# Sparse attention into a mixture of experts: loads in order of use, slots in two steps, a check moved, banks rotated

## The chip, the cores and the metric

The kernel runs on one core of one Trainium2 chip. The metric is the device time of one execution in microseconds (us): the median over several runs. The profile comes from one more execution, and its span is counted from the first to the last instruction of the program. TensorE (PE) multiplies matrices, VectorE (DVE) and ScalarE (ACT) work elementwise, GpSimd (POOL) issues gathers and scatters by index, and SyncE (SP) issues the plain transfers (DMA). PSUM, where TensorE writes, has 8 banks of 512 fp32 per partition.

## The reference

Attention of 8 batches, 8 heads, 576 positions and 64 values a head. Half of the heads look at the last 32 positions, the other half at earlier positions of the same remainder modulo 32. Its output is the input of a mixture of 8 experts, of which each token takes one:

```
scores = scale * q @ k.T;  scores = where(mask_local or mask_strided, scores, -1e9)
attn   = exp(scores - max);  attn /= sum(attn) + 1e-9;  x = attn @ v     # (8, 576, 512)
logits = x @ w_gate;  local_gate = sigmoid(x @ w_local)
for b in range(8):
    prev_e = -1
    for s in range(576):
        fresh_e = argmax(logits[b, s])
        e = fresh_e if s == 0 or local_gate[b, s] < 0.5 else prev_e
        prev_e = e
        p = softmax(logits[b, s])
        out[b, s] = p[e] * (relu(x[b, s] @ w1[e]) @ w2[e])     # w1[e]: 512 x 1024, w2[e]: 1024 x 512
```

The choice of an expert can depend on the token before it, so it is made by a scan along the tokens.

## The kernel before

The kernel has three stages. Attention works through 32 pairs of heads (8 batches of 4 pairs): scores, exponential, mask, values, then transposes for the gate. The tokens of the first three batches are routed while attention goes on ("route" with nb = 3), and six tiles of 128 tokens of them can start early as soon as attention ends. During those tiles ("early") all eight batches are routed (nb = 8); the rest follows in pairs of tiles. TensorE, VectorE, ScalarE, GpSimd and SyncE each work through their own list in order; a scheduler fixes these orders when the program is built, and `issue_after` keeps an instruction behind another one.

Queries, keys and values of a batch come in two groups of two pairs each. The queries and keys of the very first pair come in pieces; everything else of a group comes whole:

```python
    def load(b, grp):
        hs = slice(2 * grp, 2 * grp + 2)
        qt = inp.tile([P, 2, S], F32, name="qt")
        kt = inp.tile([P, 2, KW], F32, name="kt")
        if b == grp == 0:

            hq, hk = LT // 2 * LQ, LT // 2 * LQ + STRIDE
            for c, d in ((slice(0, hq), slice(0, hk)), (slice(hq, S), slice(hk, KW))):
                nc.sync.dma_start(out=qt[:, 0, c], in_=q[b][:, hs][:, 0, c])
                nc.scalar.dma_start(out=kt[:, 0, d], in_=k[b][:, hs][:, 0, d])
        a = slice(int(b == grp == 0), 2)
        nc.sync.dma_start(out=qt[:, a], in_=q[b][:, hs][:, a])
        nc.sync.dma_start(out=kt[:, a], in_=k[b][:, hs][:, a])
        st["q", b, grp], st["k", b, grp] = qt, kt
        if grp == 0:
            t = inp.tile([LK, 2, LT, VW], F32, name="vlt", bufs=2)
            nc.sync.dma_start(out=t, in_=vl[b])
        else:
            t = inp.tile([P, 2, len(SBLK), VW], F32, name="vst", bufs=2)
            nc.sync.dma_start(out=t, in_=vs[b])
        st["v", b, grp] = t

    def blocks(ap, m):
        return ap.rearrange("p h (i x) -> p h i x", i=m)
# ... cut: scores, values, transposes, gates ...
    pairs = [[Unit(b, pair, g) for g in range(2)] for b in range(B) for pair in range(PAIRS)]
    load(0, 0)
    load(0, 1)
    nc.sync.dma_start(out=wgs, in_=wg.rearrange("(k p) e -> p k e", p=P))
```

In each step n of the attention the scores of pair n are made, then route may take a step, and then come the values of pair n - 1 and the transposes of pair n - 2. Route is a generator; each `yield` gives way to the attention or the experts. Its part from the slots on (a slot is a token's place in the experts' tiles; `slot` has a row for each batch and expert, 24 or 64 of them, and a column for each position):

```python
    nc.vector.tensor_scalar(slot, cum, thr, float(SKIP), Alu.is_le if final else Alu.is_gt, Alu.mult)
    nc.vector.scalar_tensor_tensor(slot, cum, base, slot, Alu.add, Alu.add)
# ... cut ...
    nc.vector.tensor_tensor(slot, slot, hot, op=Alu.mult)
    yield


    ps = bank()
    ones = PAIR_MAX + SINGLES if final else units
    nc.tensor.matmul(ps[:, 0:ones], lhsT=c.ones, rhs=over[:, 0:ones], start=True, stop=True)
# ... cut: more small matmuls if final ...
    sp = bank()
    for t in range(LT):

        nc.tensor.matmul(sp[0:LQ, t * nb:t * nb + P], lhsT=slot[:, t * LQ:(t + 1) * LQ], rhs=c.inb[0:R],
                         start=True, stop=True)
    nc.vector.tensor_scalar(rd.et[:, 0:units], ps[0:1, 0:units], float(E - 1), None, Alu.min)
# ... cut ...
    nc.vector.tensor_tensor(rd.oh, across(c.io[:, 0:E], [P, units, E]), spread(ps[:, 0:units], [P, units, E]),
                            op=Alu.is_equal)
    sli = rp.tile([LQ, CN], I32, name="sli")
    nc.vector.tensor_copy(sli, sp[0:LQ, 0:CN])
    lo, hi = rp.tile([LQ, CN], I32, name="lo"), rp.tile([LQ, CN], I32, name="hi")
    nc.vector.tensor_scalar(lo, sli, P - 1, None, Alu.bitwise_and)
    nc.vector.tensor_scalar(hi, sli, 7, None, Alu.arith_shift_right)
    at = rp.tile([LQ, CN, n], BF16, name="at")
    nc.vector.tensor_tensor(at, across(c.io[0:LQ, 0:n], [LQ, CN, n]), spread(hi, [LQ, CN, n]), op=Alu.is_equal)
    yield
# ... cut: one-hot tables "put" and "lane" from lo, hi and at ...
    for i in range(CN):
        nc.tensor.matmul(tab, lhsT=lane[:, i], rhs=put[:, i], start=(i == 0), stop=(i == CN - 1))
# ... cut: the gathers' and scatters' row numbers, gi and si, from tab ...
```

After attention the experts take all 8 banks in a ring that starts at bank 6:

```python
    def later(self, ctx):

        self.banks = Banks(ctx.enter_context(self.tc.tile_pool(name="pse", bufs=1, space=PSUM)))
        self.banks.ring.used = 6
        xp = ctx.enter_context(self.tc.tile_pool(name="later", bufs=1))
        self.sets.append((xp.tile([P, DK, F], F32, name="w1x"), xp.tile([P, FK, D], F32, name="w2x")))
        self.xg2 = Ring(xp, 2, [P, 2, DX], "xg2")
        self.xT2 = xp.tile([P, 2, D], F32, name="xT2")
```

A unit makes its hidden layer (already begun for the first one), turns the rows of the next, and makes its output. Route takes a step after each half. The check of the attention's sums (it decides whether a careful second pass is needed) comes after five units:

```python
def bounds(tc, pool, psr, sums, bad):

    nc = tc.nc
    flat = sums.rearrange("p u h i -> p (u h i)")
    ok = pool.tile([P, B * PAIRS * 12], F32, name="ok")
    nc.vector.tensor_scalar(ok, flat, SUM_LO, None, Alu.is_ge)
    nc.vector.scalar_tensor_tensor(ok, flat, SUM_HI, ok, Alu.is_le, Alu.mult)
    low = pool.tile([P, 1], F32, name="low")
    nc.vector.tensor_reduce(low, ok, axis=AX.X, op=Alu.min)
    one = pool.tile([P, 1], F32, name="one")
    nc.vector.memset(one, 1.0)
    ps = psr.tile([P, 512], F32, name="xps")
    nc.tensor.matmul(ps[0:1, 0:1], lhsT=low, rhs=one, start=True, stop=True)
    nc.vector.tensor_scalar(bad, ps[0:1, 0:1], -1.0, float(P), Alu.mult, Alu.add)

# Experts: the end of turn_x, the turn of a unit's rows
                ins = nc.vector.tensor_copy(to[:, a], ps).ins

        pe, u["pt"] = self.pe.next(), (self.pt2 if "pair" in u else self.pt).next()
        with self.tc.issue_after(ins if n == 1 else self.rows) if n == 1 or self.rows else nullcontext():
            nc.vector.tensor_tensor(pe[:, 0:n], x[:, :, D:DX], across(u["rd"].oh[:, u["at"]], [P, n, E]), op=Alu.mult)
            nc.vector.tensor_reduce(u["pt"][:, 0:n], pe[:, 0:n], axis=AX.X, op=Alu.add)

# Experts.output
            for kk in range(FK):
                ins = nc.tensor.matmul(ps, lhsT=hT[:, kk], rhs=w2[:, kk, :], start=(kk == 0), stop=(kk == FK - 1))
        nc.scalar.activation(y, ps, Act.Copy, scale=u["pt"][:, 0:1])

    def early(self, second, check):


        def step(ins):
            with self.tc.issue_after(ins):
                next(second, None)

        for j in range(NE - 1):
            self.run(j, step)
        assert next(second, None) is None
        with self.tc.issue_after(self.end):
            check()
```

## Time and profile before

| what | value |
|---|---|
| time, median of 3 runs | 704.74 us (703.1 to 705.38) |
| span of the profiled execution | 702.4 us, mean granted TensorE clock 0.984 |
| read from and written to HBM | 159.8 and 19.5 MB, 255 GB/s over the span |
| attention, about | 5 to 170 us |
| early units, about | 170 to 260 us |
| pairs, single tiles, last pairs | 260 to 682 us |
| closing steps after the last scatter | 683 to 702 us |

How to read it: a row of the timeline or of the costliest groups has start and length in us (or busy time and mean ns), engine, line of the source, operation, and the tiles written and read. PE is a matmul, PEld the weight load that runs beside it; an fp32 matmul has two passes, and the counts are of passes. In square brackets stands how long the engine was idle just before and what ended that. The row of slices cuts the span into 40 equal parts of 17.6 us; a digit is a share in tenths, and PEclk is the clock granted to TensorE, in tenths of full speed. The view by stretches gives, for a stretch of time, the busy time of PE, PEld, DVE, ACT and POOL with the number of instructions, the granted clock, the DMA share and GB/s. The chain of waits goes back from the last instruction, at each step to what released it or to the one before it on its engine.

### The profile page before, as it was taken

To read this page: it belongs to the slowest core of one execution; us is meant where nothing else is said; L and a number is where in the kernel's file an instruction comes from. 1 tells how busy PE (TensorE), PEld (TensorE's weight loads), DVE (VectorE), ACT (ScalarE), POOL (GpSimd) and SP (SyncE) were. 2 spreads that over 40 slices of the span, in tenths; PEclk is the share of its full clock that TensorE was granted. 3 is DMA by queue.
4 is the path that set the end of the run, shared out by engine and by line. 5 is a ranking of instruction groups with operands and counts; after the bars stand their busy time and mean duration, and the time that the engine had idled before them with its cause. 6 is when DMAs were issued, how large, how long until landed. Compare 5 with 4: busy or idle time off the path is not lost.

```text
span 702.4 us, 13279 instructions
## 1 busy us (share of the span) xinstructions
PE 674.8 (96%) x5258; PEld 580.4 (83%) x5258; DVE 401.5 (57%) x901; ACT 193.1 (27%) x360; POOL 99.2 (14%) x101
## 2 busy tenths in 40 slices
PE   8999999999999999999999999999999999999980
PEld 7999889987676779999499996799999997769970
DVE  6777877773455166586437856286587551215660
ACT  3545435452111113222131322223223311113220
POOL 1000001101002421120202202121121111001210
PEclk9999989999999999999999999999999999999995
DMA  9998687995787997775768776755578767677200
GB/s 331 378 309 292 226 286 264 365 337 171 267 310 259 316 395 293 270 277 218 290 233 309 272 266 223 266 190 202 210 270 296 273 217 285 236 242 298 62 32 5
DMA packets 73626, 179.82 MB, mean 256 GB/s; under 512 B 9678, under 2 KB 19406, under 8 KB 73552
## 3 DMA queue, kind: packets, MB, share of 16 engines
q1 hardware_dynamic: 66864, 157.91, 63.4%
q0 software_dynamic: 6400, 20.63, 8.3%
q8 instruction: 45, 0.74, 0.4%
q10 hardware_dynamic: 288, 0.31, 0.2%
q14 instruction: 29, 0.24, 0.1%
HBM read 159.80 MB, written 19.55 MB: 255 GB/s over the span
## 4 chain that ended last, share of the span: by engine, by line
PE 86%; DMA 5%; DVE 4%; issue 1%; ACT 1%; SPq 1%; POOL 0%; DVEq 0%; POOLq 0%
PE bank L928 46%; PE bank L1076 10%; PE bank L1051 9%; PE vps L406 9%; PE sps L359 5%; PE bank L1072 2%; PE xps L443 2%; DMA w2t<-in_w_dram 2%; DMA w1t<-in_w_dram 1%; PE xps L460 1%; PE xps L476 1%; DMA vlt<-in_vl_dram 1%; DMA xd<-xs 1%; DVE e L366 1%; DVE xs L417 0%
## 5 line engine op out<-in xcount | busy, mean ns | idle before, releaser
L1084 POOL DMA_INDIRECT out_dram<-y,si x38 | 49.7, 1309 | 282.4 <-DVE y L996 147.4
L871 POOL DMA_INDIRECT xg<-xd,gi x42 | 46.2, 1099 | 301.4 <-DVE rc L416 151.2
L1076 PE MATMUL bank<-w2t,hT 128*128 128x512 f32 x160 | 70.7, 594 | 1.7 <-issue 1.7
L1051 PEld LDWEIGHTS bank<-xgT,w1t 128*128 128x128 f32 x576 | 65.4, 192 | 2.0 <-issue 1.7
L1051 PE MATMUL bank<-xgT,w1t 128*128 128x128 f32 x576 | 66.2, 276 | 0.0
L1076 PEld LDWEIGHTS bank<-w2t,hT 128*128 128x128 f32 x160 | 29.6, 190 | 35.0 <-issue 34.9
L963 DVE TENSOR_TENSOR part<-bank,part 128x512 f32<-128x512 f32 x13 | 9.0, 692 | 79.9 <-ACT part L960 79.9
L928 PE MATMUL bank<-xs,t 128*128 128x128 f32 x416 | 50.7, 275 | 0.0
L928 PE MATMUL bank<-t,hs 128*128 128x256 f32 x208 | 49.2, 380 | 0.2 <-DVE hs L902 0.2
L928 PEld LDWEIGHTS bank<-xs,t 128*128 128x128 f32 x416 | 48.6, 192 | 0.0
L928 PEld LDWEIGHTS bank<-xT,w1t 128*128 128x128 f32 x384 | 45.7, 192 | 2.6 <-issue 2.1
L359 PE MATMUL sps<-qt,kt 64*128 64x96 f32 (+2 forms) x704 | 46.5, 278 | 1.4 <-ACT e L363 0.7
L928 PE MATMUL bank<-xT,w1t 128*128 128x128 f32 x384 | 47.5, 276 | 0.0
L928 PE MATMUL bank<-xs,w1t 128*128 128x128 f32 x384 | 46.8, 275 | 0.0
L953 DVE TENSOR_TENSOR h<-bank,part 128x512 f32<-128x512 f32 x39 | 27.0, 691 | 34.7 <-ACT part L965 23.2
L359 PEld LDWEIGHTS sps<-qt,kt 64*128 64x128 f32 (+2 forms) x704 | 40.9, 186 | 6.0 <-issue 3.3
L928 PE MATMUL bank<-w2t,h 128*128 128x256 f32 x192 | 45.4, 380 | 0.0
L928 PE MATMUL bank<-w2t,hs 128*128 128x256 f32 x192 | 45.4, 379 | 0.0
L928 PEld LDWEIGHTS bank<-xs,w1t 128*128 128x128 f32 x384 | 44.8, 192 | 0.0
L928 PEld LDWEIGHTS bank<-t,hs 128*128 128x128 f32 x208 | 39.5, 190 | 5.8 <-issue 0.6
L993 ACT ACTIVATE part<-bank,pt 128x256 f32<-128x256 f32 x39 | 18.5, 474 | 92.4 <-PE bank L928 92.4
L363 ACT ACTIVATE e<-sps 128x576 f32<-128x576 f32 (+1 forms) x64 | 40.0, 650 | 13.9 <-PE sps L359 13.5
(283 smaller groups left out, 1125.0 us busy)
## 6 DMA issues: line engine op xcount, KB each, us to landing
w1t<-in_w_dram SPq DMA_DIRECT2D x50, 1024.0 KB
w2t<-in_w_dram SPq DMA_DIRECT2D x50, 1024.0 KB
kt<-in_k_dram SPq DMA_DIRECT2D x15, 608.0 KB
qt<-in_q_dram SPq DMA_DIRECT2D x15, 576.0 KB
vlt<-in_vl_dram SPq DMA_DIRECT2D x8, 780.0 KB
w1x<-in_w_dram SPq DMA_DIRECT2D x6, 1024.0 KB
w2x<-in_w_dram SPq DMA_DIRECT2D x6, 1024.0 KB
vst<-in_vs_dram SPq DMA_DIRECT2D x8, 650.0 KB
```

What stands on the lines that cost most here:

```text
L359: st["pe"] = nc.tensor.matmul(ps[0:kb, h, i * w:(i + 1) * w], lhsT=kt[r, u.i2, c:c + kb], rhs=qt[r, u.i2, c:c + w], start=True, stop=True)
L363: nc.scalar.activation(ev, ps[0:kb, :, 0:m * w], Act.Exp, bias=0.0, scale=1.0 / DH ** 0.5)
L406: st["end"] = nc.tensor.matmul(ps[0:w, o:o + w], lhsT=u.e[0:kb, h, i * w:(i + 1) * w], rhs=vt[0:kb, u.i2, u.t0 + i, c:c + w], start=True, ...
L443: st["end"] = nc.tensor.transpose(ps[:, i * w:(i + 1) * w], src[0:w, t, i2 * P:(i2 + 1) * P], ident[0:w, 0:w])
L871: self.nc.gpsimd.indirect_dma_start(out=u["xg"][:, a] if "pair" in u else u["xg"], out_offset=None, in_=self.xd[0:u["rows"]], in_offset=ba ...
L928: self.end = fn(*args, **kw).ins
L953: nc.vector.tensor_tensor(to, ps, add, op=Alu.add)
L993: nc.scalar.activation(to, ps, Act.Copy, scale=g[r])
L1051: ins = nc.tensor.matmul(ps[:, i * P:(i + 1) * P], lhsT=w1[:, kk, c], rhs=xT[:, kk * P:(kk + 1) * P], start=(kk == 0), stop=(kk == DK - 1))
L1072: ins = nc.tensor.matmul(ps[s], lhsT=hT[:, kk, s], rhs=w[:, kk, :], start=(kk == 0), stop=(kk == FK - 1))
L1076: ins = nc.tensor.matmul(ps, lhsT=hT[:, kk], rhs=w2[:, kk, :], start=(kk == 0), stop=(kk == FK - 1))
L1084: self.nc.gpsimd.indirect_dma_start(out=self.views[0], in_=y, in_offset=None, bounds_check=N - 1, oob_is_err=False, out_offset=bass.Indire ...
```

## The change

It has four parts. The loads of the first batch are issued pair by pair, in the order in which the attention uses them: queries and keys of a pair, then the values of the pair before it. The slots are turned back (from a row for each batch and expert to a row for each position) in two steps of three matmuls, with a step of the attention between them, where route runs beside attention; all later steps of that route move one step on. The bounds check is held behind the last VectorE operation of the last early turn of rows, so that the scheduler can't take it forward. And the ring of banks starts at 2. Careful and final variants keep their own forms.

```diff
@@ -327,23 +327,25 @@
         hs = slice(2 * grp, 2 * grp + 2)
         qt = inp.tile([P, 2, S], F32, name="qt")
         kt = inp.tile([P, 2, KW], F32, name="kt")
-        if b == grp == 0:
-
+        st["q", b, grp], st["k", b, grp] = qt, kt
+        vt = st["v", b, grp] = inp.tile([LK, 2, LT, VW] if grp == 0 else [P, 2, len(SBLK), VW], F32,
+                                        name="vst" if grp else "vlt", bufs=2)
+        src = (vs if grp else vl)[b]
+        if b:
+            nc.sync.dma_start(out=qt, in_=q[b][:, hs])
+            nc.sync.dma_start(out=kt, in_=k[b][:, hs])
+            nc.sync.dma_start(out=vt, in_=src)
+
+
+        def keys(i2):
             hq, hk = LT // 2 * LQ, LT // 2 * LQ + STRIDE
-            for c, d in ((slice(0, hq), slice(0, hk)), (slice(hq, S), slice(hk, KW))):
-                nc.sync.dma_start(out=qt[:, 0, c], in_=q[b][:, hs][:, 0, c])
-                nc.scalar.dma_start(out=kt[:, 0, d], in_=k[b][:, hs][:, 0, d])
-        a = slice(int(b == grp == 0), 2)
-        nc.sync.dma_start(out=qt[:, a], in_=q[b][:, hs][:, a])
-        nc.sync.dma_start(out=kt[:, a], in_=k[b][:, hs][:, a])
-        st["q", b, grp], st["k", b, grp] = qt, kt
-        if grp == 0:
-            t = inp.tile([LK, 2, LT, VW], F32, name="vlt", bufs=2)
-            nc.sync.dma_start(out=t, in_=vl[b])
-        else:
-            t = inp.tile([P, 2, len(SBLK), VW], F32, name="vst", bufs=2)
-            nc.sync.dma_start(out=t, in_=vs[b])
-        st["v", b, grp] = t
+            first = grp == i2 == 0
+            for c, d in (((slice(0, hq), slice(0, hk)), (slice(hq, S), slice(hk, KW))) if first else
+                         ((slice(0, S), slice(0, KW)),)):
+                nc.sync.dma_start(out=qt[:, i2, c], in_=q[b][:, hs][:, i2, c])
+                (nc.scalar if first else nc.sync).dma_start(out=kt[:, i2, d], in_=k[b][:, hs][:, i2, d])
+
+        return keys, lambda i2: nc.sync.dma_start(out=vt[:, i2], in_=src[:, i2])
 
     def blocks(ap, m):
         return ap.rearrange("p h (i x) -> p h i x", i=m)
@@ -503,8 +505,12 @@
         nc.sync.dma_start(out=xd[b * S:(b + 1) * S, D:DX].rearrange("(t p) e -> p t e", p=LQ), in_=ex)
 
     pairs = [[Unit(b, pair, g) for g in range(2)] for b in range(B) for pair in range(PAIRS)]
-    load(0, 0)
-    load(0, 1)
+
+    parts = [load(0, grp) for grp in range(2)]
+    for pair in range(PAIRS + 1):
+        for n, i in ((pair, 0), (pair - 1, 1)):
+            if 0 <= n < PAIRS:
+                parts[n // 2][i](n % 2)
     nc.sync.dma_start(out=wgs, in_=wg.rearrange("(k p) e -> p k e", p=P))
     if not careful:
 
@@ -689,11 +695,19 @@
         for h in range(2):
             nc.tensor.matmul(ps[:, ones:units], lhsT=c.half[h], rhs=whose.rearrange("e (m h) -> e h m", h=2)[:, h],
                              start=(h == 0), stop=(h == 1))
-    sp = bank()
-    for t in range(LT):
-
-        nc.tensor.matmul(sp[0:LQ, t * nb:t * nb + P], lhsT=slot[:, t * LQ:(t + 1) * LQ], rhs=c.inb[0:R],
-                         start=True, stop=True)
+    sli = rp.tile([LQ, CN], I32, name="sli")
+
+    def back(ts):
+        sp = bank()
+        for t in ts:
+
+            nc.tensor.matmul(sp[0:LQ, t * nb:t * nb + P], lhsT=slot[:, t * LQ:(t + 1) * LQ], rhs=c.inb[0:R],
+                             start=True, stop=True)
+        at = slice(ts[0] * nb, (ts[-1] + 1) * nb)
+        nc.vector.tensor_copy(sli[:, at], sp[0:LQ, at])
+
+    if final:
+        back(range(LT))
     nc.vector.tensor_scalar(rd.et[:, 0:units], ps[0:1, 0:units], float(E - 1), None, Alu.min)
     if final:
         nc.vector.tensor_copy(rd.et[:, units:], ps[0:1, units:units + 2 + NH])
@@ -704,8 +718,10 @@
         nc.vector.tensor_copy(rd.et[:, units:units + 2], cnt)
     nc.vector.tensor_tensor(rd.oh, across(c.io[:, 0:E], [P, units, E]), spread(ps[:, 0:units], [P, units, E]),
                             op=Alu.is_equal)
-    sli = rp.tile([LQ, CN], I32, name="sli")
-    nc.vector.tensor_copy(sli, sp[0:LQ, 0:CN])
+    if not final:
+        back(range(LT // 2))
+        yield
+        back(range(LT // 2, LT))
     lo, hi = rp.tile([LQ, CN], I32, name="lo"), rp.tile([LQ, CN], I32, name="hi")
     nc.vector.tensor_scalar(lo, sli, P - 1, None, Alu.bitwise_and)
     nc.vector.tensor_scalar(hi, sli, 7, None, Alu.arith_shift_right)
@@ -839,7 +855,7 @@
     def later(self, ctx):
 
         self.banks = Banks(ctx.enter_context(self.tc.tile_pool(name="pse", bufs=1, space=PSUM)))
-        self.banks.ring.used = 6
+        self.banks.ring.used = 2
         xp = ctx.enter_context(self.tc.tile_pool(name="later", bufs=1))
         self.sets.append((xp.tile([P, DK, F], F32, name="w1x"), xp.tile([P, FK, D], F32, name="w2x")))
         self.xg2 = Ring(xp, 2, [P, 2, DX], "xg2")
@@ -891,7 +907,7 @@
         pe, u["pt"] = self.pe.next(), (self.pt2 if "pair" in u else self.pt).next()
         with self.tc.issue_after(ins if n == 1 else self.rows) if n == 1 or self.rows else nullcontext():
             nc.vector.tensor_tensor(pe[:, 0:n], x[:, :, D:DX], across(u["rd"].oh[:, u["at"]], [P, n, E]), op=Alu.mult)
-            nc.vector.tensor_reduce(u["pt"][:, 0:n], pe[:, 0:n], axis=AX.X, op=Alu.add)
+            self.turned = nc.vector.tensor_reduce(u["pt"][:, 0:n], pe[:, 0:n], axis=AX.X, op=Alu.add).ins
             if "pair" in u:
                 self.sums_a(self.xs, self.blocks_x())
                 self.sums_b(self.t1, self.blocks_w(self.sets[u["set"]][0]))
@@ -1131,7 +1147,7 @@
         for j in range(NE - 1):
             self.run(j, step)
         assert next(second, None) is None
-        with self.tc.issue_after(self.end):
+        with self.tc.issue_after(self.turned):
             check()
 
     def rest(self, ctx):
```

## The prediction

> **What bounds the kernel now.** I read the page's busy shares first, then who TensorE waited for, then its timeline where it stood still, then the clock by stretches, then the chain there.

> ```profile
> PE 674.8 (96%) x5258; PEld 580.4 (83%) x5258; DVE 401.5 (57%) x901; ACT 193.1 (27%) x360; POOL 99.2 (14%) x101
> PEclk9999989999999999999999999999999999999995
> ```

> TensorE is busy 96% of the span, VectorE 57%. So only two things can pay: places where TensorE stands still, and places where it is busy but slow. The clock row has one 8, in its seventh slice (105 us on the right), far from start and end. The TensorE timeline gives the stops, in brackets, with what ended them:

> ```profile
> 7.39 1.58 PE L359 MATMUL sps<-qt,kt 64*128 64x96 f32 x24 [0.73 <-ACT e L363]
> 9.30 2.25 PE L406 MATMUL vps<-vlt,e 128*96 128x96 f32 x24 [0.33 <-DMA vlt<-in_vl_dram]
> 12.23 1.28 PE L359 MATMUL sps<-qt,kt 64*108 64x108 f32 x20 [0.69 <-issue]
> ...
> 170.56 0.60 PE L928 MATMUL xps<-ident,xg 128*128 128x128 f32 x4
> 172.89 1.10 PE L1076 MATMUL bank<-w2t,hT 128*128 128x512 f32 x2 [1.72 <-issue]
> 173.91 1.20 PE L570 MATMUL bank<-ident,codes 96*64 96x96 f32 x12
> 175.05 6.28 PE L1076 MATMUL bank<-w2t,hT 128*128 128x512 f32 x14
> ```

> Besides these, stops are small (the next largest, 0.76 us, waits for VectorE at 80.19). "Issue" means that the profile names no releaser. At 12.23 the pair is the first of the second group, whose keys are the last transfer needed. At 172.89 the VectorE and ScalarE timelines name candidates:

> ```profile
> 168.88 0.21 DVE L479 COPY lt<-xps 96x54 f32<-96x54 f32 x1 [7.77 <-PE xps L476]
> 169.86 0.36 DVE L245 TENSOR_SCALAR ok<-sums 128x384 f32<-128x384 f32 x1 [0.77 <-DMA xd<-xs]
> 170.14 0.19 DVE L482 TENSOR_REDUCE gmx<-lt 96x6 f32<-96x48 f32 x1
> ...
> 171.17 0.57 ACT L1054 ACTIVATE hT<-sps 128x512 f32<-128x512 f32 x1
> 172.14 0.65 DVE L889 COPY xgT<-xps 128x512 f32<-128x512 f32 x1
> 172.71 0.19 DVE L497 TENSOR_TENSOR codes<-code,fr 96x48 f32<-96x48 f32 x1
> ```

> ScalarE finished hT at 171.74, so it is not the last. VectorE's copy L889 ends at 172.79, 0.10 us before the matmul. The built program agrees: the first output matmul goes to bank 0, which the attention's transposes used last, and it waits for VectorE. L889 is that late because the bounds check (L245, L246, L248) had been scheduled into VectorE's queue ahead of it, and L245 itself waited 0.77 us for a store.

> Last, the clock. In the stretches below the seventh number is the granted clock, after five busy times:

> ```profile
> 99.00:100.00 1.00, 1.00 (x11) 1.00 (x10) 1.00 (x3) 0.00 (x0) 0.00 (x0) 0.99 1.04 326
> 100.00:101.00 1.00, 1.00 (x6) 0.73 (x5) 0.97 (x7) 0.00 (x0) 0.00 (x0) 0.50 0.89 368
> 106.00:107.00 1.00, 1.00 (x14) 1.00 (x14) 0.40 (x1) 0.21 (x1) 0.00 (x0) 0.59 0.23 54
> ```

> and the chain across it (start, length, what):

> ```profile
> 54.21 2.21 PE vps L406 x20
> 98.77 1.69 PE xps L695 x12
> 100.46 3.80 PE vps L406 x18
> 104.26 0.96 PE xps L443 x5
> 105.22 2.29 PE sps L359 x24
> ```

> The 20 value passes took 2.21 us at 54.21; at half clock 18 take 3.80. From the shares, 0.99 at 99 to 100 and 0.59 at 106 to 107, the slow stretch runs from 99.98 to 106.82: 6.84 us. It begins inside L695, the slots' six matmuls (12 passes) of 24 rows by 96 columns, which follow a matmul of 8 rows.

> [...] here TensorE counts as busy and stood still for only 0.16 us, so I suppose that narrow matmuls count for little. No run here shows that yet. [...] L482 started at 170.14, after L245, though its input was there at 169.09.

> **The change part by part.**

> *First loads by pair.* The bytes are the same, in order of use. Between 5 and 16.2 us the DMA moved 389 GB/s. Half of vlt (390 KB of 1024 bytes) need no longer land before the first values: 399 kB / 389 = 1.03 us earlier than 9.3, so these start when the scores end, at 8.97: 0.33 gained. Queries and keys of the third pair have the other half of vlt and the fourth pair's 288 + 304 KB no longer ahead, 982 KB in all or 2.6 us: they come at about 9.6 and are wanted at 11.2, so 0.69 is gained. What is now behind them: vlt's second half at about 10.6 (wanted 12.4), the fourth pair at 12.2 (wanted 15), both vst halves by 14 (wanted 16.3). None waits. Four more transfers cost SyncE about 4 x 0.6 us of issue; the second batch is not used before 20. The 0.73 us at 7.39 is ScalarE's and stays. Sum: 1.0.

> *Slots in two steps.* The same six matmuls, three after the next pair's scores; one more VectorE copy (0.17 us), beside other work. Later steps of the routing move one pair (some 4 us): the gather table was ready at 119.8, its rows are turned at 157.98, so that is free. The gain is the clock, if the narrow stretch is now too short to trip it. At full clock the three groups would take 18/20 x 2.21 = 1.99, 0.50 (as at 109.72) and 1.51 (as at 56.93), together 4.00; they took 7.05. With 0.2 us for the tail of L695 (1.69 against 1.48 for the later 12 passes at 205.41): 3.2 us. I give this part three chances in four.

> *Bounds check later.* Three operations, 0.36 + 0.55 + 0.54 = 1.45 us, leave the path of L479 to L497 and go to 240.5, where VectorE stood idle for 4.69 us before the check's last step. There they cost nothing.

> *Banks from 2.* In the built program the codes' matmuls (L570) now come first, into banks 2 and 3, and wait for VectorE and ScalarE; then the output's into bank 4, whose only wait is a DMA. Without the check, L497 follows L479 by six dependent steps of about 0.23 (as L490 to L492) and ends near 170.5; hT ends near 171.3, since ScalarE need not wait for a late ex. TensorE ends its transposes at 171.16, so it stops about 0.25 instead of 1.72: 1.5 gained. The scan behind them (run, lasti, hot, cum: 5.2 us from 174.73 to 179.89 in the trace) still ends before the output's 6.9 us do.

> Sum: 1.0 + 3.2 + 1.5 = 5.7 us of 704.74: 699.0.

> **Rivals.** First: the clock drops all the same[...]. It makes 702.2. Second: DMA takes the gain back. It was 94 to 110% busy from 116 to 146, and later loads have as many bytes. Against it: those loads are issued as TensorE frees their buffers, the DMA was only 23 to 46% busy in four of the six slices from 101 to 107 that the slow clock stretched, and weights landed long before use. If attention were held by transfers, the first two parts would vanish: 703. Third: the check in its new place delays the first pair's VectorE sums (from 246.19 on). They waited 0.88 us for a weight transfer there, so no: at worst 1.4 us, 700.4.

> **Range and chances.** Three in four for 699.0, one in four for about 702, with a run spread of 703.1 to 705.38 before: I say 699.3, and 697.3 to 702.5 for eight in ten. Over 2% faster would need under 690.6, and no part could do that; 2% slower has no cause in view. Within 2%: 98%.

> **What would show it.** First part: no DMA stop at the first values nor at the third pair. Second: the seventh clock slice reads 9, and value passes there take 2.2 us. Third: L479 to codes takes under 2 us, and the check stands near 240. Fourth: the stop before the codes is under 0.4 us. I'm wrong if the clock still falls once in mid-span, if a weight transfer ends a stop that was not there, or if TensorE's waits reappear after 182.

## The result, and the profile after

The changed kernel takes 701.57 us (median of 4 runs, 701.18 to 702.60) against 705.06 (4 runs, 703.10 to 705.38): a ratio of 0.9958, 95% interval 0.9937 to 0.9980. The profiled spans are 699.8 and 702.4 us. Two later comparisons gave the same two kernels ratios of 0.9909 and 0.9969, each on one chip.

The busy shares and the clock row of the page after, in the same 40 slices:

```profile
PE 672.7 (96%) x5258; PEld 577.7 (83%) x5258; DVE 402.0 (57%) x902; ACT 193.4 (28%) x360; POOL 109.3 (16%) x101
PEclk9999999999999999999999999999999999999995
```

TensorE is busy 2.1 us less, and the seventh slice reads 9. (GpSimd's 10 us more are its gathers, 1357 ns instead of 1099; the chain that ended last still gives it 0%.) Now TensorE's timeline after, at the places of the prediction and at one more:

```profile
7.09 1.58 PE L361 MATMUL sps<-qt,kt 64*128 64x96 f32 x24 [0.19 <-DMA kt<-in_k_dram]
8.60 2.28 PE L408 MATMUL vps<-vlt,e 128*96 128x96 f32 x24
10.81 1.28 PE L361 MATMUL sps<-qt,kt 64*108 64x108 f32 x20
...
98.14 2.09 PE L408 MATMUL vps<-vst,e 108*108 108x108 f32 x18
...
124.54 0.41 PE L445 MATMUL xps<-ident,xs 108*128 108x108 f32 x2 [0.24 <-issue]
125.32 0.27 PE L445 MATMUL xps<-ident,xs 126*128 126x126 f32 x1 [0.37 <-issue]
126.03 1.45 PE L361 MATMUL sps<-qt,kt 64*108 64x108 f32 x20 [0.44 <-issue]
...
169.66 1.18 PE L576 MATMUL bank<-ident,codes 96*64 96x96 f32 x12 [0.88 <-DVE pe L909]
170.77 6.70 PE L1092 MATMUL bank<-w2t,hT 128*128 128x512 f32 x15
```

The stops of 0.73, 0.33 and 0.69 us in the first 13 us have become one of 0.19. The 18 value passes after the slots take 2.09 us, not 3.87. The stop before the output is 0.88 us, not 1.72. And three stops at 124 to 126 us are new. Subtracting the start of each group of TensorE from its counterpart before gives the account: 1.42 us earlier from the third pair on, 4.45 from 106 us on, only 2.38 from 130 us on, and 3.15 at TensorE's end. So the first part gave 1.42, the clock 3.03, the stop before the output and what follows 0.77, and 2.07 were given back at 124 to 126.

That account is true of these two executions. The experiments show that it isn't how the changed kernel is faster in most.

### The profile page after: what moved, and what is told of

Its sections match the earlier page's. It is cut to its first block, busy times and chain, and to the rows that moved or that the text cites. A ratio compares the mean times of both kernels' runs of the same rounds, so it can differ in the third digit from the quotient of the medians.

```text
span 699.8 us, 13283 instructions
## 1 busy us (share of the span) xinstructions
PE 672.7 (96%) x5258; PEld 577.7 (83%) x5258; DVE 402.0 (57%) x902; ACT 193.4 (28%) x360; POOL 109.3 (16%) x101
## 4 chain that ended last, share of the span: by engine, by line
PE 90%; DVE 3%; DMA 2%; issue 1%; ACT 1%; SPq 0%; POOL 0%; DVEq 0%; POOLq 0%
PE bank L944 48%; PE bank L1092 10%; PE bank L1067 9%; PE vps L408 9%; PE sps L361 5%; PE xps L445 2%; PE bank L1088 2%; DMA w2t<-in_w_dram 2%; PE xps L462 1%; PE xps L478 1%; PE sps L1067 1%; DMA kt<-in_k_dram 1%; DVE e L368 1%; ACT e L365 0%; DVE w2t L926 0%
## 5 line engine op out<-in xcount | busy, mean ns | idle before, releaser
L887 POOL DMA_INDIRECT xg<-xd,gi x42 | 57.0, 1357 | 301.2 <-PE bank L944 128.7
```

What stands on the lines that cost most here:

```text
L887: self.nc.gpsimd.indirect_dma_start(out=u["xg"][:, a] if "pair" in u else u["xg"], out_offset=None, in_=self.xd[0:u["rows"]], in_offset=ba ...
```

## The experiments

All times are medians; each group was run on one chip with the kernel before beside it, so compare within a group. The last column is the time at half clock, averaged over the runs: 2 x (1 - mean granted clock) x span. In thirteen profiles of this kernel and its variants 14.5 to 19.0 us of it lie behind the last matmul, where no TensorE work is left to slow. The rest costs time: a straight line through the single runs of the kernel before gives 0.39, 0.45 and 0.42 us of time for each us at half clock in groups 1, 2 and 3. In the profiles before and after, the clock's changes lie a whole number of 3.413 us apart: in the first it stood at full for 95.57 us, at half for 6.83 (from 99.98 to 106.81) and at full for 580.27, in the changed kernel's at full for 675.84, which are 28, 2, 170 and 198 times that. Such a piece is called a window here.

| group | kernel | runs | us | ratio, 95% interval | half clock, us |
|---|---|---|---|---|---|
| 1 | before | 43 | 705.54 | | 23.6 |
| 1 | slots only | 22 | 704.23 | 0.9989, 0.9977 to 1.0001 | 21.7 |
| 1 | loads only | 22 | 703.57 | 0.9972, 0.9957 to 0.9986 | 22.6 |
| 1 | check and banks | 6 | 700.39 | 0.9931, 0.9911 to 0.9950 | 18.4 |
| 1 | changed kernel | 5 | 698.97 | 0.9909, 0.9888 to 0.9931 | 16.5 |
| 2 | before | 34 | 704.87 | | 24.2 |
| 2 | check only | 13 | 701.15 | 0.9942, 0.9922 to 0.9961 | 18.3 |
| 2 | banks only | 22 | 704.43 | 0.9995, 0.9981 to 1.0010 | 22.1 |
| 2 | all but slots | 6 | 698.53 | 0.9914, 0.9887 to 0.9942 | 15.8 |
| 3 | before | 53 | 703.70 | | 20.7 |
| 3 | loads and check | 16 | 700.14 | 0.9952, 0.9935 to 0.9968 | 16.8 |
| 3 | changed kernel | 22 | 701.43 | 0.9969, 0.9956 to 0.9982 | 16.7 |
| 3 | all but slots | 22 | 700.71 | 0.9949, 0.9934 to 0.9964 | 17.6 |

**Each part alone.** The kernel before with only `back` in two steps:

```diff
-    sp = bank()
-    for t in range(LT): ...            # six matmuls of the slots
+    if not final:
+        back(range(LT // 2))
+        yield
+        back(range(LT // 2, LT))
```

> The kernel before with only the slots turned back in two steps. If the parts add up: TensorE's clock stays at 1.0 through the span (no 0.5 stretch near 100 us), TensorE is about 3.0 us earlier from 107 us on and stays so to the end, about 702 us against 705. If the slots' part itself causes the new stop that the changed kernel has at 124 to 126 us (the gathers come one step later in it): the same 3.0 us at 107, but about 2 us lost again by 130, so about 704. If the place of the clock's windows decides and not the number of narrow matmuls: a half-clock stretch of 3.4 or 6.8 us is still there, and the time is about 705.

with only `load` split, and its parts called in order of use:

```diff
-    load(0, 0)
-    load(0, 1)
+    parts = [load(0, grp) for grp in range(2)]
+    for pair in range(PAIRS + 1): ...  # keys of the pair, then values of the pair before
```

> The kernel before with only the first batch loaded pair by pair. If the parts add up: stops before the first values and before the third pair's scores go, TensorE is 1.4 us earlier at the third pair and at 95 us, the half-clock stretch near 100 us stays, about 703.6 us. If the stop at 124 to 126 us comes with the loads' part: 1.4 us at 95, lost again by 130, about 705.

and with only the check and the banks (with `self.turned` set as in the change):

```diff
-        self.banks.ring.used = 6
+        self.banks.ring.used = 2
-        with self.tc.issue_after(self.end):
+        with self.tc.issue_after(self.turned):
             check()
```

> The kernel before with only the bounds check pinned and the output's banks from 2. If the parts add up: nothing changes before 165 us, the stop before the first output matmul at 171 us falls from 1.72 to 0.9 us, about 704.0. If the prediction's 1.5 us for this part was right and only the other parts disturbed it: a stop under 0.4 us, about 703.3. The check stands near 240 us in both.

The measured gains are 1.3, 2.0 and 5.2 us. The smallest term of my account is the largest alone, and at 700.39 us both expectations of the last run (704.0 and 703.3) were missed. The reason stands in VectorE's and TensorE's rows. First the kernel with only the loads changed, VectorE's timeline and then TensorE's:

```profile
164.84 0.21 DVE L481 COPY lt<-xps 96x54 f32<-96x54 f32 x1 [7.77 <-PE xps L478]
167.22 0.36 DVE L245 TENSOR_SCALAR ok<-sums 128x384 f32<-128x384 f32 x1 [2.17 <-DMA xd<-xs]
167.50 0.19 DVE L484 TENSOR_REDUCE gmx<-lt 96x6 f32<-96x48 f32 x1
```

```profile
166.52 0.60 PE L934 MATMUL xps<-ident,xg 128*128 128x128 f32 x4
170.25 2.02 PE L1082 MATMUL bank<-w2t,hT 128*128 128x512 f32 x2 [3.12 <-issue]
```

TensorE came there 4.04 us earlier than in the first profile. The transfer that L245, the check's first operation, waits for came only 2.64 us earlier. So VectorE stood 2.17 us instead of 0.77, and TensorE 3.12 instead of 1.72. And behind that standstill the clock fell to 0.50: in the stretches of the same kernel, the seventh number is again the granted clock.

```profile
168.00:169.00 1.00, 0.00 (x0) 0.00 (x0) 1.00 (x6) 0.62 (x2) 0.00 (x0) 1.00 0.84 340
169.00:170.00 1.00, 0.00 (x0) 0.00 (x0) 1.00 (x8) 0.11 (x1) 0.00 (x0) 1.00 1.03 426
170.00:171.00 1.00, 0.75 (x1) 0.47 (x2) 0.61 (x5) 0.00 (x0) 0.00 (x0) 0.64 0.60 242
171.00:172.00 1.00, 1.00 (x2) 0.00 (x0) 0.00 (x0) 0.00 (x0) 0.80 (x1) 0.50 0.29 18
```

One window, 170.28 to 173.69, ran at half clock. Of 4.04 us gained, 1.01 were left. The kernel with only the slots changed shows the longer wait too, without a fall of the clock after it: 1.92 us earlier at 153 us, a wait of 1.67, a stop of 2.63, and 1.02 left.

In the built program L245 waits in its old place for seven DMA queues, and in its new place for none; the traces have waiting instructions before it in the old place and none in the new. Its scratch comes from a pool opened when attention's pools are closed, so I read the wait as one for the stores that still read that memory; that reading is from the code.

**Check or banks.** One edit of the last pair each: only `issue_after(self.turned)`, or only `used = 2`:

```diff
-        with self.tc.issue_after(self.end):     # check only
+        with self.tc.issue_after(self.turned):
-        self.banks.ring.used = 6                # banks only
+        self.banks.ring.used = 2
```

> The kernel before with only the bounds check pinned later. If the check's wait for the stores is what holds TensorE at 165 to 172 us: the stop before the codes' matmuls is about 0.9 us, the clock does not fall after it, and the time is that of the run with both, about 700.4 us. If the banks carry the gain: a stop of 1.7 us or more, about 705 us.

> The kernel before with only the output's banks taken from 2. If the check's wait is what holds: VectorE's queue is the same, the stop is 1.7 to 3.1 us as before, 704.5 to 705.5 us. If the banks carry the gain: a stop of 0.9 us or less, about 700.5 us.

The check alone brings 3.7 us, the banks alone nothing that can be measured. TensorE's timeline with the check alone, where the ring still starts at 6:

```profile
168.09 0.60 PE L928 MATMUL xps<-ident,xg 128*128 128x128 f32 x4
169.57 1.18 PE L570 MATMUL bank<-ident,codes 96*64 96x96 f32 x12 [0.88 <-DVE pe L893]
```

The codes come first without the new banks too, so the moved check is enough for the scheduler to turn the order. With the banks alone it did not, and the rows are those of before, only worse: VectorE's wait for the store, then TensorE's stop.

```profile
168.06 0.36 DVE L245 TENSOR_SCALAR ok<-sums 128x384 f32<-128x384 f32 x1 [2.12 <-DMA xd<-xs]
```

```profile
171.08 1.10 PE L1076 MATMUL bank<-w2t,hT 128*128 128x512 f32 x2 [3.07 <-issue]
```

**Before, a second profile.** No edit.

> The kernel before with a second profile. Theory: the stop before the first output matmul is VectorE's wait for the last stores plus 0.95 us, and it is the longer, the earlier TensorE comes there; so if this execution has no half-clock stretch near 100 us, the stop is 2.5 to 3.1 us and not 1.72, and if it has one, it is 1.5 to 2.0 us. Rival: the stop belongs to the code and is 1.7 us in both cases.

VectorE's row and TensorE's:

```profile
168.24 0.36 DVE L245 TENSOR_SCALAR ok<-sums 128x384 f32<-128x384 f32 x1 [1.79 <-DMA xd<-xs]
```

```profile
171.27 1.09 PE L1076 MATMUL bank<-w2t,hT 128*128 128x512 f32 x2 [2.74 <-issue]
```

No half-clock stretch near 100 us in this one, and the stop is 2.74 us with a wait of 1.79. With the four others there are five pairs of the check's wait and TensorE's stop, beside the start of the copy that VectorE makes just before the check (L479, or L481), when TensorE has delivered its input:

| kernel | copy starts at | wait of L245 | stop of TensorE | difference |
|---|---|---|---|---|
| before, first profile | 168.88 | 0.77 | 1.72 | 0.95 |
| slots only | 166.96 | 1.67 | 2.63 | 0.96 |
| before, second profile | 166.25 | 1.79 | 2.74 | 0.95 |
| banks only | 165.73 | 2.12 | 3.07 | 0.95 |
| loads only | 164.84 | 2.17 | 3.12 | 0.95 |

The stop is the wait plus a constant, and without the check it is 0.87 to 0.88. So by this table the check's own 1.45 us of VectorE cost less than 0.1, and its wait is the loss. The earlier TensorE comes, the longer the wait: the store came 2.64 us earlier for 4.04 us of TensorE. The first profile showed the shortest wait because the half-clock stretch had made TensorE late. The second did not end earlier for having no such stretch: of 3.2 us gained at the slots, 0.7 went between 122 and 129 us, 1.0 into the longer stop and the rest later, and its last matmul ended at 682.06 us, against 681.73 in the first.

**The slots, inside the changed kernel.** The changed kernel with the slots turned back in one step, twice, and the kernel before with loads and check alone:

> The changed kernel with the slots turned back in one step, as before. If what counts is where the clock's windows lie: [...] a median about 1 us above the changed kernel's, some 700 us, with single runs up to 702.5. If one step costs a half-clock stretch of 6.8 us every time, as predicted: 3.2 us above it, about 702.2. If two steps bring nothing: the same time as the changed kernel.

> The changed kernel with the slots turned back in one step, once more, on the same chip as the changed kernel. If two steps are worth what was predicted: 3.2 us slower than the changed kernel. If they are worth only the executions in which a clock window falls on the slots: up to 1 us slower, with single runs 2 us above the rest. If nothing: the same.

> The kernel before with the first loads pair by pair and the bounds check pinned; slots in one step, banks as before. If these two parts are the whole gain: the time of the changed kernel, about 698.8 us, a stop of 0.9 us at 167 us. If slots or banks add something once the check is gone: 1 us or more above the changed kernel.

The first two undo one part of the changed kernel, the third leaves out two:

```diff
-        back(range(LT // 2))                # all but slots, twice
-        yield
-        back(range(LT // 2, LT))
+        back(range(LT))
-        self.banks.ring.used = 2            # loads and check: this too
+        self.banks.ring.used = 6
```

One step, 698.53 us in group 2 (0.9914) and 700.71 in group 3, is no slower than two (0.9909 in group 1; 701.43 in group 3). In group 3 two steps are 0.7 us slower, with intervals that overlap; that they cost time as a whole isn't shown, but a gain of 3.2 us is excluded. On TensorE they do cost a little: from 97 to 113 us the other eight profiles with one step gain 3.18 to 3.20 us on the first profile, the three of the changed kernel 3.02 to 3.03. So with the clock whole the old single step already has the 3.2 us that the prediction gave to the change. Loads and check alone reach 700.14 beside the changed kernel's 701.43. Of nine profiles with the slots in one step only the first shows the half clock there. Of four with two steps one does, the kernel with only the slots changed:

```profile
98.00:99.00 1.00, 0.84 (x7) 0.68 (x6) 1.00 (x4) 0.16 (x1) 0.00 (x0) 1.00 0.97 395
99.00:100.00 1.00, 1.00 (x7) 0.97 (x7) 1.00 (x5) 0.00 (x0) 0.00 (x0) 0.59 1.02 420
101.00:102.00 1.00, 1.00 (x7) 1.00 (x7) 0.83 (x3) 0.00 (x0) 0.00 (x0) 0.50 0.50 51
```

Its half-clock window runs from 99.18 to 102.59, and its clock row on the page reads 9 in that slice all the same: 3.41 us at half in a slice of 17.6 make a mean of 0.90.

**What halves the clock.** A kernel of matmuls alone; attention and experts are left out.

```python
STAGES = ((24, 96), (48, 96), (52, 96), (56, 96), (64, 96), (64, 128), (96, 48), (128, 48), (128, 24))
for rows, cols in STAGES:
    for r, c, count in ((128, 128, 140), (rows, cols, 180)):
        for i in range(count):
            nc.tensor.matmul(ps[0:c, 0:P], lhsT=a[0:r, 0:c], rhs=x[0:r], start=True, stop=True)
```

> TensorE alone: nine stretches of 180 back-to-back matmuls of r rows by c columns, each after 140 matmuls of 128 rows by 128 columns; attention and experts are left out. Theory: the clock falls [...] under 55 rows, and columns don't matter: the stretches of 24, 48 and 52 rows by 96 columns show a clock of 0.5, those of 56 and 64 rows by 96 columns, and 96 or 128 rows by 24 or 48 columns stay at 1.0. Rival 1, rows times columns [...]: all but the stretch of 64 rows by 128 columns fall. Rival 2, only standstill counts: none falls, as TensorE never stops.

The clock row of its page (slices of 17.8 us, stages from left to right), and then its groups by shape, with the mean of one pass behind the comma:

```profile
PEclk9965558965559999999999999999999999999999
```

```profile
L100 PE MATMUL pp<-x,a 48*96 48x128 f32 x360 | 71.6, 396 | 0.0
L100 PE MATMUL pp<-x,a 24*96 24x128 f32 x360 | 71.6, 395 | 0.0
...
L100 PE MATMUL pp<-x,a 52*96 52x128 f32 x360 | 39.5, 269 | 0.0
...
L100 PE MATMUL pp<-x,a 64*96 64x128 f32 x360 | 39.5, 269 | 0.0
L100 PE MATMUL pp<-x,a 128*48 128x128 f32 x360 | 39.5, 273 | 0.0
...
L100 PE MATMUL pp<-x,a 128*24 128x128 f32 x360 | 39.5, 273 | 0.0
```

TensorE never stops here. With 24 or 48 rows its clock falls and stays at half for the whole stretch; with 52 rows or more it doesn't, and few columns do no harm: the granted clock is 0.50 from 50 to 70 us (24 rows) and from 150 to 170 (48 rows), and 1.00 from 250 to 280 (52 rows), and at 24 columns of 128 rows a pass takes 273 ns against 395 and 396. In these shapes rows count and columns don't; the limit lies between 48 and 52 of 128, lower than the 55 that I had taken from the other traces, whose shares rest on modelled ends of matmuls. So matmuls of few rows brought the clock to 0.50 without a stop, much as the prediction supposed.

In the kernel the slots' six matmuls in one step brought it down in one profile of nine. What follows on the windows is my estimate from the traces: I cut TensorE's time, in the thirteen profiles, into the windows of 3.413 us that the clock's own changes fix, and weighted the busy time by rows / 128, since rows alone counted above. Of about 2500 windows at full clock up to 676 us, three were followed by half clock: two at the slots, at shares of about 0.4, and one at 0.085 (the stop of 3.12 us). Of those that stayed, one was just under 0.4 and all others at 0.43 or more. These shares rest on the modelled ends, so they give no sharp limit. Moving such a window over the traces gives an estimate of the chances: with the slots in one step some four in ten of its positions hold a share under 0.43, with two steps less than one in ten, and a stop of 2.6 to 3.1 us makes it two thirds to four fifths at the output, one of 1.72 or 0.88 none. The windows lay differently from profile to profile (full clock began between 4.4 and 7.3 us, at 4.41 in the first and 4.91 in the changed kernel's), but not evenly: it began between 6.0 and 6.6 us in eight of the thirteen, where by the same estimate the slots' stretch is spared and the output's is at the edge or inside.

**The new stop at 124 us.** The changed kernel without an edit, profiled a second and a third time:

> The changed kernel again, with a second profile. If the stop of TensorE, ScalarE and SyncE at 124 to 126 us belongs to the program: it is there again, TensorE loses about 2 us there, the profiled span is about 699.8. If it was an accident of one execution: no such stop, the profiled span is about 697.7 and the timed median stays near 701.5.

> The changed kernel once more, a third profile. If the stop of several engines at 124 to 126 us in its first profile is rare: it is not there, and TensorE ends near 676.5 to 678.5 us. If it belongs to the program: it is there in two of three profiles, at 2 us.

It is absent from the second profile (group 1) and there in the third (group 3), with stops of 0.37, 0.42 and 0.46. The second profile was no faster for it: its span is 699.6 us, where 697.7 was expected without the stop, since TensorE waited 1.26 and 0.93 us for VectorE at 323.67 and 342.90. In none of the nine profiles with one step does TensorE stop more than 0.29 us there, nor in the one with only the slots changed. ScalarE in the third profile, then GpSimd:

```profile
122.18 0.65 ACT L365 ACTIVATE e<-sps 128x576 f32<-128x576 f32 x1 [0.77 <-PE sps L361]
126.03 0.65 ACT L365 ACTIVATE e<-sps 128x576 f32<-128x576 f32 x1 [3.19 <-PE vps L408]
```

```profile
119.75 1.14 POOL L887 DMA_INDIRECT xg<-xd,gi  x1 [115.85 <-DVE rc L418]
121.19 0.95 POOL L887 DMA_INDIRECT xg<-xd,gi  x1 [0.30 <-issue]
122.45 0.95 POOL L887 DMA_INDIRECT xg<-xd,gi  x1 [0.30 <-issue]
123.70 0.95 POOL L887 DMA_INDIRECT xg<-xd,gi  x1 [0.30 <-issue]
```

ScalarE's two exponentials belong to one pair, whose scores ended at 121.9, yet the second starts 3.2 us after the first ended; SyncE's next load starts at 126.02 too. They stand while GpSimd issues the last two of the four gathers, which two steps have moved a pair later, and 1.4 us beyond. With one step the gathers lie at 115.88 to 120.78 in the second profile with all but the slots (group 3); ScalarE's second exponential is late there as well, by 1.57 us. By the starts of its matmuls TensorE lost 0.68 to 0.72 us between 121 and 130 us in each of the three one-step profiles of group 3 and 2.0 in the two-step one, and nothing in the seven profiles of groups 1 and 2. So the loss goes with the group (another chip, at another time) as well as with the gathers' place; why three engines stand around them stays open. A version with the gathers elsewhere wasn't tried.

## Why the prediction was right, and where it wasn't

The time was right: 701.57 in a range of 697.3 to 702.5, and within 2%, though the gain was 3.5 us where the sum was 5.7. The way to it was partly luck.

*First loads by pair:* right. No stop at the first values or at the third pair, 1.42 us where 1.0 was predicted; the 0.73 us at 7.39, said to stay, fell to 0.19. But 1.42 is the largest of seven: at the third pair the profiles with these loads stand 0.46 to 1.42 us ahead of the first profile, the others -0.18 to 0.53, and the means differ by 0.9. Alone the part measured 2.0 us, with an interval of 1.0 to 3.0. That the pieces land in the order in which they are issued, on which the sum rested, was my estimate; the traces show only that the stops of 0.33 and 0.69 us went with the new order.

*Slots in two steps:* this failed. The mechanism was right (narrow matmuls, 6.83 us at half clock, 3.03 us in the profile for 3.2 predicted), but the term was sized as if every execution had this stretch. One profile in nine with one step has it. Alone it measured 1.3 us with an interval that reaches no change, and inside the changed kernel nothing. The sentence that later steps move one pair, "so that is free", failed too in the two profiles where the gathers' new place came with a stop that gave back about 2 us. The rival that the clock drops all the same was seen once, in the kernel with only the slots changed.

*Bounds check later:* the term is missing from the prediction's sum as its own, and is the largest. I priced its 1.45 us of VectorE and the stop of 1.72 us as one profile showed it. The wait of 0.77 us for a store stood in the lines that I showed; I didn't ask what becomes of it when the other two parts bring TensorE there earlier. It grows, to 2.17 us, and the stop with it, until at a stop of 3.12 us the clock falls to 0.50 behind it. So executions without the half clock at the slots lost part of that time here instead: 1.0 of 3.2 us in the second profile of the kernel before, 3.0 of 4.04 with only the loads changed. With the check moved the half-clock time falls from 24.2 to 18.3 us a run, 5.9 us, worth up to 2.9 of the 3.7 us measured (2.7 by the line fitted in group 2); that the rest is the shorter stop is likely and not shown, as the two overlap. The check stands at 239.58, as predicted. In three profiles of group 3 its matmul then held TensorE for about 0.5 us, which "there they cost nothing" overlooks.

*Banks from 2:* failed as a cause. The stop fell to 0.88 and not to 0.25, with the ring at 2 as with it at 6: the codes' matmuls come 0.15 us after VectorE's copy of xgT (168.82 to 169.51), which starts as TensorE's transposes end and takes 0.69 us; the prediction had timed the stop by the codes and by ScalarE's hT, which ended at 168.24 and 168.99. Nor was the old stop shown to be a wait for bank 0: with the banks alone the first output matmul goes to another bank and still starts 0.10 us after that copy. The expected end of VectorE's chain was right (codes ended at 168.24, 1.74 us after L481 began).

*The rivals of DMA and of the check on the first pair* did not come: the profile names no transfer as the end of the new stop.

*What would show it:* the clock row could not have shown it, as one halved window still reads 9.

No variant was clearly faster than the changed kernel. Loads and check, two of the four parts, reached as much as all four in group 3.

## What to carry to other kernels

A wait for something that does not come earlier by as much, such as the store's landing here (2.64 us earlier for 4.04 us of TensorE), is not a cost of its present size: it swallows part of what is gained ahead of it, so ask of each wait on the path how it grows if the engine comes earlier, and remove it first. A half-clock stretch in one profile need not be in the next: with the slots in one step, one profile in nine had it near 100 us. Weigh it by how often it comes, and look at the granted clock of all runs before pricing it. Parts of a change that act on one path must be run one at a time and together, and beside the old kernel each time: 1.3, 2.0 and 5.2 us alone made 6.6 together in group 1, and the whole change 2.3 in group 3.
